# Channel mix of a fused three-stage kernel: where its operand parts are made, when its loads are issued, and the place of one relu

## The chip, the cores and the metric

The kernel runs on one core of a Trainium2 chip. The metric is the time of one execution on the device in microseconds (us), as the median of three runs. The engines are named as the profile names them: PE is TensorE's matmuls and PEld its weight loads, DVE is VectorE, ACT is ScalarE, SP is SyncE, whose queue issues nearly all DMAs. Each engine runs its own instructions in the order in which they were written for it, and waits where an operand of another engine, or a buffer, isn't there yet.

## The reference

Three layers in a row, all float32. The batch is 4 sequences of 3072 tokens, the model width 256.

```python
attn = np.maximum((1 / 3072) * z @ z.T, 0) ** 2          # d_qk 64
x = u * (attn @ v)
h = x @ w_in                                             # 256 -> 2048
x = (h - np.tanh(h)) @ w_out                             # 2048 -> 256
x_prev = x shifted by one token in its sequence, zero ahead of the first
xk = mu_k * x + (1 - mu_k) * x_prev
xr = mu_r * x + (1 - mu_r) * x_prev
k = np.maximum(xk @ w_k, 0)                              # 256 -> 1024
out = 1 / (1 + np.exp(-(xr @ w_r))) * (k * k @ w_v)      # 1024 -> 256
```

The last five lines are the channel mix.

## The kernel before

**Precision.** Every float32 operand of a matmul is held as two parts: a high part h, which ScalarE (line 87) or VectorE makes by a copy that rounds, and a low part l = value - h, which VectorE makes (line 90). A product is three matmuls: high times high, high times low, low times high (`PASSES`).

**Tiling.** Tokens go in 24 tiles of 512, features in chunks of 128. The channel mix takes two tiles at a time, t0 = 2i and t1 = 2i + 1, in 12 **groups**. A group is four **units** (j = 0 to 3, one `h_unit` each, called unit 0 to unit 3 here) and then an **r slot** (`r_slot`), 24 matmuls for the sigmoid's argument. Hidden products are made by a Winograd scheme: the four operands "own" B11, B12, B21, B22 (two tiles by two chunks of xk) and the differences T1 to T4 stand against weights A11, A12, S1 to S4 and -A22, seven products a unit. Of the operands, B11, T1, B22, T3, B21, T2 and T4 are needed as parts; B12 goes only into differences.

**A unit on TensorE** (line 724 the seven products, line 761 the pieces of the second matmul, against w_v, of the unit before): A11 x B11 into bank `wa`, A12 x B21 into bank `we`, a third of the pieces, S2 x T2, S1 x T1, more pieces, S4 x B22, S3 x T3, the rest of the pieces, and last -A22 x T4 on top of `wa`. Units 0 to 3 have 39, 45, 51 and 45 matmuls, the r slot 24: 204 a group.

**What stands between them.** ScalarE copies `wa` after A11 x B11 (`r<-wa`), VectorE adds `we` to it (line 824). ScalarE splits off the high part of the previous unit's hidden values (`h_Hy`), VectorE the low part (`l_Hy`). ScalarE copies `wa` and `we` after S2 and S1 (line 730, into `rc`). Then `run_steps` puts the **steps** that are due into VectorE's order, then `later_load` tasks issue DMAs. Then come VectorE's two additions of `we` and `wa` to `rc` (line 853), after S4 and S3: -A22 x T4 writes into `wa`, so TensorE can't start it before the second addition has read `wa`. Then `l_Hx`, and on ScalarE relu and square of `rc` (lines 740, 741) and of `wa` after -A22 x T4.

**The steps.** For each group, `k_groups` prepares the next group's operands in five lists, one for each unit and one for the r slot: `own` is a multiply-add on two loaded tiles (line 422), `minus` a difference (line 438), `part` a high copy on ScalarE and the low part on VectorE. `r_step` prepares xr for the group that is running: line 422, a copy (483) and a difference (90), one step in each unit. Two tiles of output of the group before are transposed (`out_turn`, line 928) and sent in eight DMAs each (line 934), the odd tile out of `ends` in unit 3, the even one as a step of the r slot. `mix_load` (lines 416, 417) loads the two tiles of an `own` or an `r_step`, one slot ahead; in the r slot the loads were written behind the steps.

**Queues and buffers.** All these DMAs go through SyncE's queue in the order written. A load waits for a free buffer, and every DMA takes one of eight completion counters in turn, so it also waits until the eighth DMA before it has landed.

Of the kernel before, what the change touches and what calls it, by code (L numbers as in the profile page):

```python
# [19 lines left out]
def relu2_attention__tanh_ffn__channel_mix_kernel(  # L20
# [406 lines left out]
    def k_groups(i):  # L427
# [13 lines left out]
        def part(n):  # L441
            t = st.pop(n)
            if n in ("B11", "B21"):
                if "h" not in st:
                    st["h"], st["l"] = p4(f"kh{i}", F32R), p4(f"kl{i}", F32R)
                k = 0 if n == "B11" else 1
                h, l = st["h"][:, k], st["l"][:, k]
            elif n == "B22" or not i:
                w = p4(f"kp{i}_{n}", F32R)
                h, l = w[:, 0], w[:, 1]  # L450
            else:
                key, k = ("T2", 0) if n == "T2" else ("T2", 1) if n == "T1" else ("T3", int(n == "T4"))
                key = "big" + key
                if key not in st:
                    st[key] = big(f"kt{i}_{key}").rearrange("p (b l t) -> p b l t", b=2, l=2)
                h, l = st[key][:, k, 0], st[key][:, k, 1]
            copy_hi(h, t)
            sub_lo(l, t, h)
            x[n] = (h, l)

# [6 lines left out]
        def q(n):  # L467
            return (0.7, lambda: part(n))

        return [  # L470
            [o("B11", t0, 0), o("B12", t1, 0), d("T1", "B12", "B11", True)],
            [q("B11"), o("B22", t1, 1), d("T3", "B22", "B12")],
            [d("T2", "B22", "T1", True), q("B22"), q("T1")],
            [q("T3"), o("B21", t0, 1), d("T4", "T2", "B21", True)],
            [q("T2"), q("B21"), q("T4")],
        ]
# [335 lines left out]
    def h_unit(n, q):  # L812
# [12 lines left out]
        if n:  # L825
            low = h_split("y")
            if "a" in hb:
                less(gx[:, 0], hb.pop("a"))
            low()
        if L == "H":  # L830
            tanh(gx[:, 1], r1)
            less(gx[:, 1], r1)
# [12 lines left out]
        for f in lates.pop(slot(n), ()):  # L845
            f()
# [10 lines left out]
        empty()  # L857
        if L == "H":
            tanh(gy, rc)
            less(gy, rc)  # L860
        else:
            relu2(gy, rc)
        hb["y"] = (n, 0, 2, ((n, 0, 1), (n, 1, 1)), gy)
        product(a, n, "-A22", "T4", False, True)
        if L == "H":
            tanh(gx[:, 0], a)
            hb["a"] = a
        else:
            relu2(gx[:, 0], a)
            for f in ends.pop(slot(n), ()):  # L870
                f()

    def h_end(n):
        gx = hb["g"][0]
        h_split("y")()
        hb["x"] = (n, 0, 1, ((n - 1, 1, 0), None), gx)
        h_split("x")()

    def r_slot(i, between):
# [13 lines left out]
        between()  # L893
        for t in (2 * i, 2 * i + 1):
# [57 lines left out]
    ends = {}  # L952
# [100 lines left out]
    for i in range(NT // 2):  # L1053
        n = NB + (NK + 1) * i
        first = n - NK - 1 if i else n - 8
        groups = {}

        def group(k, i=i, groups=groups):
            if not groups:
                groups["g"] = k_groups(i)  # L1060
            return groups["g"][k]

        for k in range(5):
            for t, c in ([(2 * i, 0), (2 * i + 1, 0)], [(2 * i + 1, 1)], [], [(2 * i, 1)], [])[k]:
                later_load(first + k - 1, mix_load, 0, t, c)
            task(first + k, first + k, group, k)
        for k in range(4):
            later_load(n + k - 1, mix_load, 1, 2 * i + k // 2, k % 2)
            task(n + k, n + k, lambda t, c: [(1.9, lambda: r_step(t, c))], 2 * i + k // 2, k % 2)
        n += NK + 1  # L1070
        if i < NT // 2 - 1:
            ends[n + 3] = [lambda c=c, t=2 * i + 1: out_turn(t, c) for c in range(DC)]
            task(n + 4, n + 4, lambda t: [(0.7, lambda c=c: out_turn(t, c)) for c in range(DC)], 2 * i)
# [25 lines left out]
    with tc.manual_schedule():  # L1099
# [45 lines left out]
        for n, (L, i, j) in enumerate(seq):  # L1145
# [4 lines left out]
            if L == "K" and j == NK - 1:  # L1150
# [4 lines left out]
                run_steps(m)  # L1155
                for f in lates.pop(m, ()):
                    f()
        n = len(seq) - 1
# [36 lines left out]
```

## Time and profile before

| | |
|---|---|
| median of 3 runs | 2628.63 us (2621.77 to 2632.17) |
| profiled execution | 2623.51 us |
| its span, first to last instruction | 2621.7 us |
| busy in the span: TensorE, VectorE, ScalarE | 96%, 75%, 69% |
| share of the chain that ended last: TensorE, VectorE, ScalarE, DMA | 15%, 4%, 2%, 2% |

The page gives one execution. Busy times are shares of the whole span, with three stages in it: attention up to about 950 us, the tanh layer up to about 1924 us, and the channel mix. In 40 slices of the span TensorE shows 9 (90% or more) up to slice 31 and 8 in the last nine, which lie in the channel mix. The engine rows of a stage are therefore read for that stage alone. In a timeline row the number in brackets is how long the engine sat idle before the row, and whose work ended that. A matmul's row is 0.39 us long while another starts every 0.23 us, since they overlap.

### The profile page before, as it was taken

How to read it: one execution, taken by the hardware profiler on the slowest of the kernel's cores; microseconds unless marked ns; L12 is line 12 of the kernel's file. 1: busy time of each engine (PE TensorE's matmuls, PEld its weight loads, DVE VectorE, ACT ScalarE, POOL GpSimd, SP SyncE). 2: the span in 40 equal slices, each digit the busy share in tenths (PEclk: the TensorE clock that was granted, in tenths of full speed). 3: DMA queues.
4: the chain of work that ended last, by engine and by line, in shares of the span. 5: the costliest groups of instructions: out<-in, count | busy, mean ns of one | idle time of the engine just before them, and what ended most of it. 6: DMA issues, size and time to landing. Idle time of an engine off the chain costs nothing. (4 is left out here: it accounts for less than half of the span.)

```text
span 2621.7 us, 30656 instructions
## 1 busy us (share of the span) xinstructions
PE 2523.3 (96%) x10907; PEld 2064.0 (79%) x10907; DVE 1974.1 (75%) x2650; ACT 1820.9 (69%) x2424; POOL 0.7 (0%) x5
## 2 busy tenths in 40 slices
PE   9999999999999999999999999999999888888888
PEld 7888888888888887888888888888877666676666
DVE  8888888888788777777777777777776666666665
ACT  7766875776687666676776776767777666666665
POOL 0000000000000000000000000000000000000000
PEclk9999999999999999999999999999999999999999
DMA  7798689679868931012110111102232333322233
GB/s 191 219 233 216 204 222 237 187 203 227 212 211 268 232 118 37 29 65 97 65 49 17 65 65 65 49 19 87 101 129 59 96 117 87 97 81 81 81 91 71
DMA packets 425145, 326.06 MB, mean 124 GB/s; under 512 B 270624, under 2 KB 344352, under 8 KB 424992
## 3 DMA queue, kind: packets, MB, share of 16 engines
q1 hardware_dynamic: 419712, 323.45, 43.3%
q8 instruction: 85, 1.39, 0.2%
q10 hardware_dynamic: 5280, 0.66, 0.2%
q14 instruction: 68, 0.56, 0.1%
HBM read 182.45 MB, written 135.54 MB: 121 GB/s over the span
## 5 line engine op out<-in xcount | busy, mean ns | idle before, releaser
L708 PE MATMUL acc_A<-h_A,v 128*128 128x512 f32 x1344 | 441.0, 390 | 0.0
L573 ACT ACTIVATE a_A<-w_A 128x1024 f32<-128x1024 f32 (+1 forms) x169 | 172.7, 1022 | 199.9 <-PE w_A L667 199.2
L708 PE MATMUL acc_A<-h_t,v 128*128 128x512 f32 x960 | 310.0, 389 | 0.0
L708 PEld LDWEIGHTS acc_A<-h_A,v 128*128 128x128 f32 x1344 | 253.1, 188 | 52.4
L761 PE MATMUL acc_H<-h_Hy,w_out 128*128 128x512 f32 x768 | 263.9, 389 | 0.0
L708 PE MATMUL acc_A<-l_A,v 128*128 128x512 f32 x672 | 262.4, 390 | 0.2 <-DVE l_A L90 0.2
L761 PE MATMUL acc_H<-h_Hx,w_out 128*128 128x512 f32 x768 | 252.2, 389 | 0.0
L90 DVE TENSOR_TENSOR l_A<-a_A,h_A 128x1024 fp32r<-128x1024 f32 (+1 forms) x169 | 201.8, 1194 | 64.4 <-ACT h_A L87 63.6
L724 PE MATMUL wa<-xo_T,w_in 128*128 128x512 f32 x864 | 243.4, 390 | 2.3 <-DVE rc L853 2.1
L824 DVE TENSOR_TENSOR r<-we,r 128x512 f32<-128x512 f32 x144 | 99.4, 690 | 155.9 <-PE we L724 86.6
L601 DVE STREAM_TRANSPOSE k<-a_A 128x512 f32<-128x512 f32 x240 | 155.9, 688 | 76.1 <-ACT a_A L574 75.4
L708 PEld LDWEIGHTS acc_A<-h_t,v 128*128 128x128 f32 x960 | 180.2, 188 | 37.4
L730 ACT ACTIVATE rc<-wa 128x512 f32<-128x512 f32 x144 | 86.0, 597 | 159.1 <-PE wa L724 159.0
L724 PEld LDWEIGHTS wa<-xo_T,w_in 128*128 128x128 f32 x864 | 161.6, 188 | 38.1 <-DVE rc L853 4.7
L708 PE MATMUL acc_A<-l_t,v 128*128 128x512 f32 x480 | 186.7, 389 | 0.0
L90 DVE TENSOR_TENSOR l_Hy<-g_H,h_Hy 128x1024 fp32r<-128x1024 f32 x144 | 175.6, 1219 | 9.7 <-ACT h_Hy L87 9.2
L574 ACT ACTIVATE a_A<-a_A 128x1024 f32<-128x1024 f32 (+1 forms) x169 | 178.4, 1056 | 5.4
L90 DVE TENSOR_TENSOR l_Hx<-g_H,h_Hx 128x1024 fp32r<-128x1024 f32 (+1 forms) x145 | 175.0, 1207 | 3.2 <-ACT h_Hx L87 3.0
L87 ACT ACTIVATE h_t<-b 128x512 fp32r<-128x512 f32 x240 | 137.1, 619 | 57.7 <-PE acc_A L708 53.7
L724 PE MATMUL wa<-kt_bigT,w_k 128*128 128x512 f32 x396 | 122.5, 420 | 55.9 <-DVE rc L853 55.9
L734 ACT ACTIVATE g_H<-rc 128x1024 f32<-128x1024 f32 x96 | 101.9, 1062 | 105.4 <-DVE rc L853 105.4
L761 PEld LDWEIGHTS acc_H<-h_Hy,w_out 128*128 128x128 f32 x768 | 144.2, 188 | 30.0 <-ACT h_Hy L87 0.2
(211 smaller groups left out, 5500.6 us busy)
## 6 DMA issues: line engine op xcount, KB each, us to landing
at<-k SPq DMA_DIRECT2D x120, 512.0 KB, 3.8
b<-at SPq DMA_DIRECT2D x240, 256.0 KB, 6.4
prevd<-pv SPq DMA_DIRECT2D x96, 256.0 KB, 2.3
mx<-x2d SPq DMA_DIRECT2D x96, 256.0 KB, 3.9
my<-prevd SPq DMA_DIRECT2D x96, 256.0 KB, 4.2
vr<-in_v_dram SPq DMA_DIRECT2D x24, 512.0 KB, 6.8
uin<-in_u_dram SPq DMA_DIRECT2D x192, 64.0 KB, 2.7
x1d<-uT SPq DMA_DIRECT2D x24, 512.0 KB, 3.4
```

Source lines behind the costliest of these rows:

```text
L87: nc.scalar.activation(out=o, in_=i, func=ACTF.Copy)
L90: nc.vector.tensor_tensor(out=o, in0=i, in1=hi.bitcast(F32), op=ALU.subtract)
L573: nc.scalar.activation(out=a[:, x], in_=w[:, x], func=ACTF.Relu, scale=sc)
L574: nc.scalar.activation(out=a[:, x], in_=a[:, x], func=ACTF.Square)
L601: nc.vector.transpose(out=t[:, :, :, c].rearrange("p b a j -> p a b j"), in_=a[:, c].rearrange("p (a b i) -> p a b i", a=4, b=4),)
L708: nc.tensor.matmul(o[c], w[j][a][:, c * P : (c + 1) * P], s[m][:, j], start=p == 0 and j == 0 and n == 0, stop=p == last and j == 1 and n ...
L724: nc.tensor.matmul(o, w[l][:, (j % 4) * P : (j % 4 + 1) * P], x[m], start=first and k == 0, stop=last and k == 2, skip_group_check=True,)
L730: nc.scalar.activation(out=t, in_=a, func=ACTF.Copy)
L734: nc.scalar.activation(out=g, in_=h, func=ACTF.Tanh)
L761: nc.tensor.matmul(o[c], w[a][:, f % 4, c * P : (c + 1) * P], hp[n, half, t][m], start=bool(first and k == 0), stop=bool(last and k == 2),)
L824: nc.vector.tensor_tensor(out=r1, in0=e, in1=r1, op=ALU.add)
```

## The change

1. `part` becomes `high` and `low`. The high copies of a unit are written behind its steps and its loads, ahead of `h_Hx`'s copy (`starts`); the low parts behind VectorE's two additions and `l_Hx` (`ends`). Parts are made in units 1, 2 and 3 (B11 and T1; B22 and T3; B21, T2 and T4), none in the r slot.
2. The differences go ahead: T3 and T2 in unit 1, T4 in unit 2. So three lists of steps remain in place of five, and the loads for them move with them.
3. `r_step`s: of the four, the first goes to the r slot before the group, and unit 1 has none (the first group keeps one in each unit).
4. The odd tile's transposes become steps of unit 3, ahead of the additions, with their eight DMAs. In the r slot the loads are written ahead of the steps, so ahead of the even tile's output transfers.
5. Relu and square of `wa` are written one unit later, behind `r<-wa` and `h_Hy`'s copy.

```diff
-        def part(n):
-            t = st.pop(n)
+        def high(n):
+            t = st[n]
...
             copy_hi(h, t)
-            sub_lo(l, t, h)
             x[n] = (h, l)
+
+        def low(n):
+            sub_lo(x[n][1], st[n], x[n][0])
...
         return [
             [o("B11", t0, 0), o("B12", t1, 0), d("T1", "B12", "B11", True)],
-            [q("B11"), o("B22", t1, 1), d("T3", "B22", "B12")],
-            [d("T2", "B22", "T1", True), q("B22"), q("T1")],
-            [q("T3"), o("B21", t0, 1), d("T4", "T2", "B21", True)],
-            [q("T2"), q("B21"), q("T4")],
-        ]
+            [o("B22", t1, 1), d("T3", "B22", "B12"), d("T2", "B22", "T1", True)],
+            [o("B21", t0, 1), d("T4", "T2", "B21", True)],
+            [],
+        ], high, low
...
             low()
+            if "relu" in hb:
+                relu2(gx[:, 0], hb.pop("relu"))
...
         run_steps(slot(n))
-        for f in lates.pop(slot(n), ()):
+        for f in lates.pop(slot(n), []) + starts.pop(slot(n), []):
             f()
...
         empty()
+        for f in ends.pop(slot(n), []):
+            f()
...
         else:
-            relu2(gx[:, 0], a)
-            for f in ends.pop(slot(n), ()):
-                f()
+            hb["relu"] = a
...
-        first = n - NK - 1 if i else n - 8
+        first = n - NK - 1 if i else n - 7
...
-        for k in range(5):
-            for t, c in ([(2 * i, 0), (2 * i + 1, 0)], [(2 * i + 1, 1)], [], [(2 * i, 1)], [])[k]:
+        for k in range(4):
+            for t, c in ([(2 * i, 0), (2 * i + 1, 0)], [(2 * i + 1, 1)], [(2 * i, 1)], [])[k]:
                 later_load(first + k - 1, mix_load, 0, t, c)
-            task(first + k, first + k, group, k)
-        for k in range(4):
-            later_load(n + k - 1, mix_load, 1, 2 * i + k // 2, k % 2)
-            task(n + k, n + k, lambda t, c: [(1.9, lambda: r_step(t, c))], 2 * i + k // 2, k % 2)
+            if k < 3:
+                task(first + k, first + k, group, k)
+            for x in ((), ("B11", "T1"), ("B22", "T3"), ("B21", "T2", "T4"))[k]:
+                starts.setdefault(first + k, []).append(lambda x=x, g=groups: g["g"][1](x))
+                ends.setdefault(first + k, []).append(lambda x=x, g=groups: g["g"][2](x))
+        for k, m in enumerate((-1, 0, 2, 3) if i else (0, 1, 2, 3)):
+            later_load(n + m - 1, mix_load, 1, 2 * i + k // 2, k % 2)
+            task(n + m, n + m, lambda t, c: [(1.9, lambda: r_step(t, c))], 2 * i + k // 2, k % 2)
         n += NK + 1
         if i < NT // 2 - 1:
-            ends[n + 3] = [lambda c=c, t=2 * i + 1: out_turn(t, c) for c in range(DC)]
-            task(n + 4, n + 4, lambda t: [(0.7, lambda c=c: out_turn(t, c)) for c in range(DC)], 2 * i)
+            for t, m in ((2 * i + 1, n + 3), (2 * i, n + 4)):
+                task(m, m, lambda t: [(0.7, lambda c=c: out_turn(t, c)) for c in range(DC)], t)
...
                 r_slot(i, lambda: h_end(n + 1) if final else None)
-                run_steps(m)
                 for f in lates.pop(m, ()):
                     f()
+                run_steps(m)
```

TensorE's order is the same in both kernels. The others are shown at three places of a middle group. Numbers in the names are those of the hidden products' units, counted through both layers (115 is unit 3 of a group, 116 and 117 are units 0 and 1 of the next), and of tiles (t = 6 to 13).

VectorE, from unit 3's `l_Hx` through the r slot to unit 0, before: the transposes `ot`, and low parts (line 90, `kt`, `kl`) that wait for ScalarE's copies.

```order
L90 TENSOR_TENSOR l_Hx115_17879<-g_H_8381,h_Hx115_17878 128x1024
L928 STREAM_TRANSPOSE ot7_17906<-sg7_17534 128x512 x2
L928 STREAM_TRANSPOSE ot6_17951<-sg6_17531 128x512
L90 TENSOR_TENSOR kt5_bigT2_17786<-kd5_T2_17781,kt5_bigT2_17786 128x512
L928 STREAM_TRANSPOSE ot6_17951<-sg6_17531 128x512
L90 TENSOR_TENSOR kl5_17693<-my0_10_1_17794,kh5_17692 128x512
L90 TENSOR_TENSOR kt5_bigT3_17872<-kd5_T4_17876,kt5_bigT3_17872 128x512
L824 TENSOR_TENSOR r1_116_17988<-we_116_17980,r1_116_17988 128x512
L90 TENSOR_TENSOR l_Hy115_17992<-g_H_8381,h_Hy115_17991 128x1024
L422 SCALAR_TENSOR_TENSOR my1_10_0_17969<-mx1_10_0_17968,head_63,my1_10_0_17969 128x512
```

VectorE at the same place now: the three low parts stand directly behind `l_Hx`, a first r step (`my1_10_0`, `mr10`) between the even tile's transposes.

```order
L90 TENSOR_TENSOR l_Hx115_17897<-g_H_8381,h_Hx115_17896 128x1024
L90 TENSOR_TENSOR kl5_17705<-my0_10_1_17701,kh5_17704 128x512
L90 TENSOR_TENSOR kt5_bigT2_17707<-kd5_T2_17694,kt5_bigT2_17707 128x512
L90 TENSOR_TENSOR kt5_bigT3_17799<-kd5_T4_17791,kt5_bigT3_17799 128x512
L931 STREAM_TRANSPOSE ot6_17973<-sg6_17541 128x512
L422 SCALAR_TENSOR_TENSOR my1_10_0_17890<-mx1_10_0_17889,head_63,my1_10_0_17890 128x512
L481 CAST mr10_17979<-my1_10_0_17890 128x512
L90 TENSOR_TENSOR mr10_17979<-my1_10_0_17890,mr10_17979 128x512
L931 STREAM_TRANSPOSE ot6_17973<-sg6_17541 128x512
L822 TENSOR_TENSOR r1_116_17996<-we_116_17988,r1_116_17996 128x512
L90 TENSOR_TENSOR l_Hy115_18000<-g_H_8381,h_Hy115_17999 128x1024
```

Both tiles' transposes and all low parts stood between `l_Hx115` and `r1_116` before; one tile's transposes and the first r step have taken the others' place.

SyncE's queue around the same r slot, before: 16 output DMAs, then the loads.

```order
L934 DMA out_0_dram<-ot7_17906 32x16x32 x8
L934 DMA out_0_dram<-ot6_17951 32x16x32 x8
L416 DMA mx1_10_0_17968<-x2d10_98 128x512
L417 DMA my1_10_0_17969<-prevd1_1_120 128x512
L416 DMA mx0_12_0_17972<-x2d12_100 128x512
L417 DMA my0_12_0_17973<-prevd0_2_117 128x512
L416 DMA mx0_13_0_17976<-x2d13_101 128x512
L417 DMA my0_13_0_17977<-prevd0_2_117 128x512
```

SyncE's queue there now, with the odd tile's transfers (`ot7`) from unit 3 and the even tile's (`ot6`) from the r slot:

```order
L937 DMA out_0_dram<-ot7_17875 32x16x32 x8
L416 DMA mx1_10_0_17889<-x2d10_98 128x512
L417 DMA my1_10_0_17890<-prevd1_1_120 128x512
L416 DMA mx1_10_1_17961<-x2d10_98 128x512
L417 DMA my1_10_1_17962<-prevd1_1_120 128x512
L416 DMA mx0_12_0_17965<-x2d12_100 128x512
L417 DMA my0_12_0_17966<-prevd0_2_117 128x512
L416 DMA mx0_13_0_17969<-x2d13_101 128x512
L417 DMA my0_13_0_17970<-prevd0_2_117 128x512
L937 DMA out_0_dram<-ot6_17973 32x16x32 x8
```

Eight output DMAs (the odd tile's, written in unit 3) stand ahead of the eight loads, and eight (the even tile's) behind them.

VectorE in unit 1, before: between `l_Hy` and the two additions (`rc`, line 853) stand an r step, a low part, an own operand, a difference and two multiplications for the output.

```order
L90 TENSOR_TENSOR l_Hy116_18073<-g_H_8381,h_Hy116_18072 128x1024
L422 SCALAR_TENSOR_TENSOR my1_10_1_18026<-mx1_10_1_18025,head_63,my1_10_1_18026 128x512
L483 CAST mr10_18017<-my1_10_1_18026 128x512
L90 TENSOR_TENSOR mr10_18017<-my1_10_1_18026,mr10_18017 128x512
L90 TENSOR_TENSOR kl6_18107<-my0_12_0_17973,kh6_18106 128x512
L422 SCALAR_TENSOR_TENSOR my0_13_1_18030<-mx0_13_1_18029,head_63,my0_13_1_18030 128x512
L438 TENSOR_TENSOR my0_13_0_17977<-my0_13_1_18030,my0_13_0_17977 128x512
L919 TENSOR_TENSOR sg8_17945<-acc_K8_17747,sg8_17945 128x512 x2
L853 TENSOR_TENSOR rc_117_18090<-we_117_18061,rc_117_18090 128x512
L853 TENSOR_TENSOR rc_117_18090<-wa_117_18062,rc_117_18090 128x512
```

VectorE in unit 1 now:

```order
L90 TENSOR_TENSOR l_Hy116_18074<-g_H_8381,h_Hy116_18073 128x1024
L422 SCALAR_TENSOR_TENSOR my0_13_1_18033<-mx0_13_1_18032,head_63,my0_13_1_18033 128x512
L438 TENSOR_TENSOR my0_13_0_17970<-my0_13_1_18033,my0_13_0_17970 128x512
L438 TENSOR_TENSOR kd6_T2_18108<-my0_13_1_18033,kd6_T1_18030 128x512
L922 TENSOR_TENSOR sg8_17955<-acc_K8_17756,sg8_17955 128x512 x2
L853 TENSOR_TENSOR rc_117_18093<-we_117_18062,rc_117_18093 128x512
L853 TENSOR_TENSOR rc_117_18093<-wa_117_18063,rc_117_18093 128x512
L90 TENSOR_TENSOR l_Hx117_18124<-g_H_8381,h_Hx117_18123 128x1024
L90 TENSOR_TENSOR kl6_18119<-my0_12_0_17966,kh6_18118 128x512
L90 TENSOR_TENSOR kt6_bigT2_18121<-kd6_T1_18030,kt6_bigT2_18121 128x512
```

The r step and the low part are gone from there, a second difference (`kd6_T2`) has come in; the low part of B11 (`kl6`) and that of T1 behind it come after `l_Hx117`.

## Rows read from the trace of the kernel before

**Rows 1.** Waits of TensorE, 1973.1 to 2599.2 us: total us, times, longest.

```profile
PE wa L724 <- DVE rc L853: 55.9, 30, 4.7
PE we L724 <- ACT kh L87: 11.5, 11, 1.0
PE we L724 <- DVE kl L90: 9.3, 11, 0.9
```

**Rows 2.** Engines by stretch: us, busy (instructions) of each, granted clock, DMA share, GB/s.

```profile
1973.10:2599.20 626.10, 549.42 (x2245) 435.83 (x2244) 417.85 (x592) 417.33 (x604) 0.00 (x0) 0.96 0.30 85
```

**Rows 3.** Timeline, TensorE, one group: start, us, line, tiles, count, [idle before <-releaser].

```profile
2206.25 0.39 PE L724 MATMUL wa<-kh,w_k 128*128 128x512 f32 x1
...
2208.13 0.50 PE L724 MATMUL we<-kh,w_k 128*128 128x512 f32 x1 [1.04 <-ACT kh L87]
2209.53 0.49 PE L724 MATMUL we<-kl,w_k 128*128 128x512 f32 x1 [0.90 <-DVE kl L90]
...
2221.74 0.97 PE L724 MATMUL wa<-kt_bigT,w_k 128*128 128x512 f32 x3 [3.04 <-DVE rc L853]
...
2234.18 0.96 PE L724 MATMUL wa<-kt_bigT,w_k 128*128 128x512 f32 x3 [1.90 <-DVE rc L853]
2234.98 0.40 PE L724 MATMUL wa<-kh,w_k 128*128 128x512 f32 x1
...
2245.89 0.84 PE L724 MATMUL wa<-kt_bigT,w_k 128*128 128x512 f32 x3
...
2256.97 0.96 PE L724 MATMUL wa<-kt_bigT,w_k 128*128 128x512 f32 x3 [0.72 <-DVE rc L853]
```

**Rows 4.** Timeline, SyncE's queue, output transfers of the same group.

```profile
2201.68 9.19 SPq L934 DMA_DIRECT2D out_dram<-ot  x16
```

**Rows 5.** DMA issues by line: count, KB each, median us from issue to landing.

```profile
my<-prevd SPq DMA_DIRECT2D x96, 256.0 KB, 4.2
```

**Rows 6.** Timeline, VectorE, same group: r slot, units 0 and 1.

```profile
2200.95 1.89 DVE L928 STREAM_TRANSPOSE ot<-sg 128x512 f32<-128x512 f32 x3
...
2215.28 0.75 DVE L422 SCALAR_TENSOR_TENSOR my<-mx,head,my 128x512 f32<-128x512 f32 x1 [2.94 <-DMA my<-prevd]
...
2219.00 0.75 DVE L422 SCALAR_TENSOR_TENSOR my<-mx,head,my 128x512 f32<-128x512 f32 x1 [1.05 <-DMA my<-prevd]
2219.79 0.69 DVE L438 TENSOR_TENSOR kd_T<-my,my 128x512 f32<-128x512 f32 x1
2220.40 0.68 DVE L853 TENSOR_TENSOR rc<-we,rc 128x512 f32<-128x512 f32 x1
2221.00 0.68 DVE L853 TENSOR_TENSOR rc<-wa,rc 128x512 f32<-128x512 f32 x1
...
2225.53 0.69 DVE L824 TENSOR_TENSOR r<-we,r 128x512 f32<-128x512 f32 x1 [1.52 <-ACT r L730]
2226.48 1.23 DVE L90 TENSOR_TENSOR l_Hy<-g_H,h_Hy 128x1024 fp32r<-128x1024 f32 x1 [0.26 <-ACT h_Hy L87]
2227.62 0.75 DVE L422 SCALAR_TENSOR_TENSOR my<-mx,head,my 128x512 f32<-128x512 f32 x1
...
2229.66 0.69 DVE L90 TENSOR_TENSOR kl<-my,kh 128x512 fp32r<-128x512 f32 x1
...
2232.85 0.68 DVE L853 TENSOR_TENSOR rc<-we,rc 128x512 f32<-128x512 f32 x1
```

**Rows 7.** Timeline, ScalarE, same group.

```profile
2207.46 0.62 ACT L87 ACTIVATE kh<-my 128x512 fp32r<-128x512 f32 x1
...
2223.77 0.58 ACT L740 ACTIVATE g_H<-wa 128x512 f32<-128x512 f32 x1
...
2224.92 0.58 ACT L730 ACTIVATE r<-wa 128x512 f32<-128x512 f32 x1
...
2234.16 1.06 ACT L740 ACTIVATE g_H<-rc 128x1024 f32<-128x1024 f32 x1 [3.59 <-DVE rc L853]
...
2256.95 1.06 ACT L740 ACTIVATE g_H<-rc 128x1024 f32<-128x1024 f32 x1 [2.39 <-DVE rc L853]
```

More of the change, by code (lines that the diff above doesn't have):

```diff
@@ L451, in part @@
             else:
-                key, k = ("T2", 0) if n == "T2" else ("T2", 1) if n == "T1" else ("T3", int(n == "T4"))
-                key = "big" + key
+                key = "big" + ("T2" if n in ("T1", "T2") else "T3")
                 if key not in st:
                     st[key] = big(f"kt{i}_{key}").rearrange("p (b l t) -> p b l t", b=2, l=2)
+                k = int(n in ("T1", "T4"))
                 h, l = st[key][:, k, 0], st[key][:, k, 1]
             copy_hi(h, t)
-            sub_lo(l, t, h)
             x[n] = (h, l)
+        def low(n):
+            sub_lo(x[n][1], st[n], x[n][0])
         def o(n, t, c):
@@ L465, in d @@
             return (0.7, lambda: minus(*y))
-        def q(n):
-            return (0.7, lambda: part(n))
         return [
             [o("B11", t0, 0), o("B12", t1, 0), d("T1", "B12", "B11", True)],
-            [q("B11"), o("B22", t1, 1), d("T3", "B22", "B12")],
-            [d("T2", "B22", "T1", True), q("B22"), q("T1")],
-            [q("T3"), o("B21", t0, 1), d("T4", "T2", "B21", True)],
-            [q("T2"), q("B21"), q("T4")],
-        ]
+            [o("B22", t1, 1), d("T3", "B22", "B12"), d("T2", "B22", "T1", True)],
+            [o("B21", t0, 1), d("T4", "T2", "B21", True)],
+            [],
+        ], high, low
     def r_step(t, c):
@@ L875, in h_end @@
         h_split("y")()
+        relu2(gx[:, 0], hb.pop("relu"))
         hb["x"] = (n, 0, 1, ((n - 1, 1, 0), None), gx)
@@ L893, in r_slot @@
         between()
+        if "relu" in hb:
+            relu2(hb["g"][0][:, 0], hb.pop("relu"))
         for t in (2 * i, 2 * i + 1):
@@ L951, in relu2_attention__tanh_ffn__channel_mix_kernel @@
     at = {x: n for n, x in enumerate(units)}
-    ends = {}
+    starts, ends = {}, {}
     loads, tasks = {}, []
@@ L1060, in group @@
                 groups["g"] = k_groups(i)
-            return groups["g"][k]
-        for k in range(5):
-            for t, c in ([(2 * i, 0), (2 * i + 1, 0)], [(2 * i + 1, 1)], [], [(2 * i, 1)], [])[k]:
+            return groups["g"][0][k]
+        for k in range(4):
+            for t, c in ([(2 * i, 0), (2 * i + 1, 0)], [(2 * i + 1, 1)], [(2 * i, 1)], [])[k]:
                 later_load(first + k - 1, mix_load, 0, t, c)
-            task(first + k, first + k, group, k)
-        for k in range(4):
-            later_load(n + k - 1, mix_load, 1, 2 * i + k // 2, k % 2)
-            task(n + k, n + k, lambda t, c: [(1.9, lambda: r_step(t, c))], 2 * i + k // 2, k % 2)
+            if k < 3:
[6 more added lines that the diff above has]
+            task(n + m, n + m, lambda t, c: [(1.9, lambda: r_step(t, c))], 2 * i + k // 2, k % 2)
         n += NK + 1
         if i < NT // 2 - 1:
-            ends[n + 3] = [lambda c=c, t=2 * i + 1: out_turn(t, c) for c in range(DC)]
-            task(n + 4, n + 4, lambda t: [(0.7, lambda c=c: out_turn(t, c)) for c in range(DC)], 2 * i)
+            for t, m in ((2 * i + 1, n + 3), (2 * i, n + 4)):
+                task(m, m, lambda t: [(0.7, lambda c=c: out_turn(t, c)) for c in range(DC)], t)
     tasks.sort(key=lambda x: x[:3])
```

## The prediction

> **What bounds the kernel now.** I read the page's slices first: TensorE is the full engine until the channel mix, and only there not. So I took that stage alone, from the first r slot to the last, 11 groups in 626.1 us, and asked in the waits view whom TensorE waits for in it [rows 1]: 55.9 us in 30 waits for VectorE's additions to `rc`, and 11.5 and 9.3 us in 11 waits each for B21's high and low part. VectorE and ScalarE are busy for 418 and 417 us of the 626, 38 us a group [rows 2], so neither is short of time; they are late at certain places. The timeline of one group shows which [rows 3]. In unit 0 A12 x B21 waits 1.04 us for `kh` and 0.90 us for `kl` (b); -A22 x T4 waits 3.04 us in unit 0 (c), 1.90 us in unit 1 (d), none in unit 2 (the row at 2245.89), 0.72 us in unit 3 (a).
>
> The stage's floor: from 2234.98 to 2245.89 TensorE starts 48 matmuls without a wait [rows 3], 0.2273 us each. 204 of them are 46.4 us a group, 510.1 us for eleven. The stretch has 116.0 us more. 76.7 us of it are the waits of rows 1. A wait's row starts at the modelled end of a matmul 0.39 us long, 0.16 us after the next could have started: 52 times 0.16 is 8.3 us. The mean granted clock is 0.96 [rows 2]; 4% of 626 us is 25 us, which stretches at 1.2 instead of 2.4 GHz take. 6 us are left, some 0.1 us of slow start behind each wait.
>
> **The change part by part,** in us from a unit's first matmul. Matmul m of a unit starts at 0.2273 x (m - 1), and its result is there some 0.45 us later (0.39 from [rows 3], and a short signal).
>
> (b) B21, T2 and T4 are parts of the r slot now. Their copies stand behind ScalarE's sigmoids (`kh`'s at 2207.46, 1.2 us after unit 0 has begun [rows 7]). In the new order they are made in unit 3: three copies of 0.62 us [rows 7] ahead of `h_Hx`, three low parts behind `l_Hx`. There ScalarE sits idle for 2.39 us ahead of `rc`'s relu [rows 7], and two copies come in addition, 1.24 us. The additions end at 8.5 there (as in unit 1, below), `h_Hx` somewhat later, `l_Hx` takes 1.2 and three low parts 1.8: the parts are ready some 12 us after unit 3's start, and unit 0 needs the first 45 + 24 matmuls after it, at 15.7. Both waits go.
>
> (c) In unit 0 VectorE waits 2.94 us for a load of the r step and 1.05 us for one of `own` [rows 6]. SyncE issues 16 output transfers for 9.19 us first [rows 4], and the loads stand behind them; a load lands 4.2 us after its issue [rows 5]. Now only two loads, those of the r step in the r slot, are behind eight outputs of unit 3; these end about 9.1 us after unit 3's start, so the loads land at about 14, and VectorE reaches that step at about 13. One us of waiting there has cover, since VectorE needs 0.63 us (a third of 1.89 [rows 6]) and 2.04 us for what is left in the r slot, and its next work for TensorE, `r`'s addition, can't begin before A12 x B21 is done, 1.6 us into unit 0, at 17.3. The other six loads follow by 12.7 and are wanted from 19.3 to 22: even at twice 4.2 us the last is there at 21.1. So no load is late. But the steps of unit 0 stay: an r step 2.04 (2227.62 to 2229.66), two `own` of 0.79 and a difference of 0.61 (2219.00 to 2220.40 [rows 6]), 4.2 in all. Unit 0's `r<-wa` starts when A11 x B11 is done, 0.9; with 0.58 for it [rows 7] and 1.05 for the `h_Hy` copy, `l_Hy` starts at 2.5 and takes 1.14 (2226.48 to 2227.62): the steps begin at 3.65 and end at 7.85. From the first addition to -A22 x T4 it is 1.34 (2220.40 to 2221.74 [rows 3, 6]), so TensorE can go on at 9.2; its 37th matmul could have started at 8.2. One us of wait stays, and I allow 0.1 for the slow start: 1.1 in place of 3.04 + 0.16 + 0.1.
>
> (d) In unit 1, 5.23 us of VectorE's order lie between the end of `l_Hy` and the first addition (2227.62 to 2232.85 [rows 6]). The r step goes (2.04) and so does `kl` (0.6), a difference comes (0.61): 3.2. Relu and square of `wa` take 1.15 us of ScalarE ahead of `r<-wa` (2223.77 to 2224.92 [rows 7]), and VectorE's `r` addition, `l_Hy` and steps hang on that copy (1.52 us of waiting at 2225.53); behind the copy they hold up nothing that TensorE wants within the unit. So the additions could come 3.2 us earlier. They are then bound by S3 x T3, the 33rd matmul, done at 7.75; with the second addition and its signal 8.5, and the 43rd matmul is due at 9.55. The wait of 1.90 goes, with 1.0 to spare. The low parts of this unit fall behind `l_Hx`, where VectorE had waited 1.52 us and more for `r<-wa`; two of 0.6 fit. ScalarE's two copies, one more than before, have 3.59 us of idle time (2234.16 [rows 7]).
>
> (a) In unit 3 two transposes of 0.63 us stand where a low part with its wait, an `own` and a difference stood, and ScalarE comes 1.15 us earlier: more than the 0.72 that is missing. Their eight transfers are issued while SyncE has nothing else due.
>
> Unit 2 has an `own` in place of two low parts ahead of its additions; it has no wait now and gets none.
>
> The sum: ten groups of the eleven prepare a successor and keep 1.1 us; the last has only (b), and keeps nothing. What was due to the clock goes with the waits that came before it; in rows 3 even the 1.90 us wait is followed by 48 matmuls at full speed, so I count none for one of 1 us. 116.0 - 10 x 1.1 = 105 us. For the first group, beside the tail of the tanh layer, I count nothing; as ScalarE has other work there, a gain there is between nothing and the 10 us of a steady group. The profiled execution took 2623.5 us: 2518.5 by this sum. Its time is 5.1 us below the median, 2628.6, so I put the median after at **2523 us**.
>
> **The rivals.**
> - *Loads still hold unit 0.* Eight loads in a row and eight outputs each wait until the eighth transfer before has landed, and for a buffer. If the six loads come late, (c) stays as it is. Of the 55.9 us, 7.2 are (a) and 19.0 (d), ten times each; 29.7 are left for (c), 31.3 with the 0.16, and with them about half of the 25 us of the clock. 2523 - 11 + 31 + 12 = 2555 us. For it: SyncE is a single queue in order. Against it: the 21.1 worked out above, and 19.3 as the first need.
> - *ScalarE becomes late.* Its copies stand ahead of `h_Hx` in units 1 to 3, which moves `h_Hx` to about 9.1 in unit 3, 0.7 behind the additions, and relu of `rc` and the next `r<-wa` with it. If all of that reached TensorE, 0.7 x 3 x 11 = 23 us: 2546 us. Against it: 38 us of work a group [rows 2] in 47.5.
> - *Slower.* The first r step of the next group is now in the r slot, ahead of `r`'s addition and `l_Hy` of unit 0 in VectorE's order, and its load is the first behind eight outputs. If it lands late, everything of unit 0 is late. From 0.6 us on (17.3 less 14 of arrival and 2.67 of work) each us costs ten a run. To end at 2642, 13 us slower than before, it must be 12.5 us late ((2642 - 2523) / 10 + 0.6), a landing of some 17 us against 4.2 [rows 5]; at 15 us late it would be 2523 + 144 = 2667 us.
> - *No change.* The wait may be one for room: `we`, `wa` and the loads rotate through few buffers, and an order that makes the same things earlier only waits for the same rooms. Then the time stays at 2629 us. Against it: in unit 1 VectorE works without a pause from 2227.62 up to the addition that TensorE waits for [rows 6]; what ends the wait is work. The Trainium skill ("Perfetto Trace Analysis", Optimization Strategy) says that consistent bubbles, the same gap repeating, can mean that there isn't enough SBUF or PSUM for the next tile. By that rule this change would give nothing; these rows speak for order, not for room.
>
> **How the numbers follow.** The forecast gets 0.70, loads that hold unit 0 0.15, a late ScalarE 0.08, no change 0.04, slower 0.03. A measurement of this kernel can tell about 0.5% from no change, 13 us. Forecast, loads and ScalarE are all faster by more: 0.93; same 0.04; slower 0.03. The forecast's own range is 2509 (no wait left in unit 0, and some gain in the first group) to 2541 (half of the second case); the two next cases end at 2555, and with the spread of the runs I take 2509 to 2558.
>
> **What would show it.** In the profile after: no TensorE wait for `kh` or `kl` in unit 0; at most one wait for `rc` a group, in unit 0, near 1 us, where the waits view now has 55.9 us; groups of about 47.5 us between r slots in place of 57; granted clock near 1.00 in the stage; VectorE waiting for no load in unit 0; `r<-wa` directly behind the square of `rc`. Wrong would be: waits for `my<-prevd` in the r slot of more than 2 us, `rc` waits in units 1 to 3, or a clock that stays at 0.96 though the waits are gone.

## The result, and the profile after

| | before | after |
|---|---|---|
| median (4 runs each) | 2629.07 us | 2514.72 us (2512.92 to 2517.76) |
| profiled execution | 2623.51 us | 2512.92 us |
| its span | 2621.7 us | 2511.1 us |
| first to last r slot | 626.1 us | 517.0 us |
| busy: TensorE, VectorE, ScalarE | 96%, 75%, 69% | 99%, 79%, 73% |

The ratio is 0.957, 95% interval 0.9548 to 0.9593. The forecast was 2523 us, from 2509 to 2558.

The waits of TensorE in the stretch from the first r slot to the last, which answer [rows 1] (line 853 is still the additions; line 722 is the products):

```profile
PE wa L722 <- DVE rc L853: 5.2, 10, 0.5
```

The same stretch by engine, which answers [rows 2] (start and end; busy us of PE, PEld, DVE, ACT, POOL; granted clock, DMA share, GB/s):

```profile
1973.00:2490.00 517.00, 511.83 (x2246) 420.42 (x2245) 422.30 (x592) 418.19 (x600) 0.00 (x0) 1.00 0.38 103
```

Of 76.7 us of waits 5.2 are left, one of 0.5 us in each of ten groups; VectorE and ScalarE are about as busy as they were (418 and 417 us before), and the granted clock went from 0.96 to 1.00. TensorE's unit 0 of the group whose r slot starts at 2161.28, which answers [rows 3]:

```profile
2166.72 0.39 PE L722 MATMUL wa<-kh,w_k 128*128 128x512 f32 x1
...
2174.66 0.39 PE L759 MATMUL acc_K<-h_Hy,w_v 128*128 128x512 f32 x1
2175.56 0.97 PE L722 MATMUL wa<-kt_bigT,w_k 128*128 128x512 f32 x3 [0.52 <-DVE rc L853]
```

VectorE in the r slot and in that unit 0, which answers [rows 6]:

```profile
2161.89 1.29 DVE L90 TENSOR_TENSOR kt_bigT<-kd_T,kt_bigT 128x512 fp32r<-128x512 f32 x2
...
2164.60 0.75 DVE L422 SCALAR_TENSOR_TENSOR my<-mx,head,my 128x512 f32<-128x512 f32 x1 [0.80 <-DMA my<-prevd]
...
2168.35 0.69 DVE L822 TENSOR_TENSOR r<-we,r 128x512 f32<-128x512 f32 x1 [1.19 <-PE we L722]
2169.18 1.23 DVE L90 TENSOR_TENSOR l_Hy<-g_H,h_Hy 128x1024 fp32r<-128x1024 f32 x1
2170.32 0.75 DVE L422 SCALAR_TENSOR_TENSOR my<-mx,head,my 128x512 f32<-128x512 f32 x1
...
2172.18 1.41 DVE L422 SCALAR_TENSOR_TENSOR my<-mx,head,my 128x512 f32<-128x512 f32 x2
2173.61 0.69 DVE L438 TENSOR_TENSOR kd_T<-my,my 128x512 f32<-128x512 f32 x1
2174.22 0.68 DVE L853 TENSOR_TENSOR rc<-we,rc 128x512 f32<-128x512 f32 x1
2174.82 0.68 DVE L853 TENSOR_TENSOR rc<-wa,rc 128x512 f32<-128x512 f32 x1
```

From 2169.18 to the second addition VectorE has no gap: the wait that is left for TensorE is for VectorE's work in unit 0. SyncE's queue around this r slot, which answers [rows 4] (the six loads between 2161.02 and 2163.82 are left out):

```profile
2155.41 4.96 SPq L937 DMA_DIRECT2D out_dram<-ot  x8
2160.42 0.51 SPq L416 DMA_DIRECT2D mx<-x2d  x1
...
2163.82 0.42 SPq L417 DMA_DIRECT2D my<-prevd  x1
2164.34 6.86 SPq L937 DMA_DIRECT2D out_dram<-ot  x8
```

All eight loads are out before the even tile's outputs. Groups are 47.07 us apart (2161.28 to 2208.34), where they were 53.6 to 58.8, and 46.24 for the last, which prepares no successor, where it was 50.4.

The one place without a gain is the first group, which lies ahead of the first r slot: that starts at 1973.0, as before (1973.1). The waits of TensorE from 1905 to there, first before, then after:

```profile
PE wa L724 <- DVE rc L853: 5.6, 4, 2.7
```

```profile
PE wa L722 <- DVE rc L853: 3.8, 2, 3.0
PE acc_K L759 <- ACT x L907: 2.0, 1, 2.0
```

### The profile page after: what moved, and what is told of

Its sections match the earlier page's. It is cut to its first block, busy times and chain, and to the rows that moved or that the text cites. A ratio compares the mean times of both kernels' runs of the same rounds, so it can differ in the third digit from the quotient of the medians.

```text
span 2511.1 us, 30719 instructions
## 1 busy us (share of the span) xinstructions
PE 2485.2 (99%) x10907; PEld 2048.1 (82%) x10907; DVE 1978.5 (79%) x2650; ACT 1823.9 (73%) x2424; POOL 0.7 (0%) x5
## 4 chain that ended last, share of the span: by engine, by line
PE 92%; DVE 3%; DMA 2%; ACT 1%; SPq 1%; issue 1%; DVEq 0%; ACTq 0%
PE acc_A L706 31%; PE acc_H L759 20%; PE wa L722 15%; PE we L722 11%; PE acc_K L759 7%; PE w_A L665 3%; PE w_A L664 3%; DMA out_dram<-ot 1%; DVE my L422 1%; SPq L937 1%; PE wa_r L889 1%; PE we_r L889 1%; DVE rc L853 1%; DMA mx<-x2d 0%; DMA my<-prevd 0%
## 5 line engine op out<-in xcount | busy, mean ns | idle before, releaser
L853 DVE TENSOR_TENSOR rc<-we,rc 128x512 f32<-128x512 f32 x144 | 99.1, 688 | 106.4 <-PE we L722 104.0
```

The lines of the kernel that those rows point to most:

```text
L853: nc.vector.tensor_tensor(out=rc[:, k], in0=x, in1=rc[:, k], op=ALU.add)
```

## Experiments: the change with one part undone

A kernel's ratio is to the kernel before, measured in the same series on the same chip. To see what an undone part costs, compare with 2514.72 us and with the 517.0 us between the r slots. The kernel before took from 2629.07 to 2632.67 us in the four series, so a difference of a few us between medians of two series shows nothing by itself; there the distance of the groups in the trace decides. Two parts of the change were not undone alone: the differences that go ahead, and the odd tile's transposes.

**Loads behind the outputs again.**

```diff
-                for f in lates.pop(m, ()):
-                    f()
                 run_steps(m)
+                for f in lates.pop(m, ()):
+                    f()
```

> The changed kernel, but in the r slot the loads are written behind the steps again, so six loads stand behind the even tile's eight outputs. Theory (c: the loads behind outputs held unit 0): in the profile after, these outputs take SyncE from 2164.3 to 2171.2, so the six loads are issued 2171.2 to 2174.0 in place of 2161.5 to 2164.2 and land some 4 us later; unit 0's steps end 3 to 5 us later, and its one wait for rc grows from 0.68 to 3 to 6 us. Ten times that and some lost clock: 2545 to 2580 us. Rival (the loads had cover anyway, moving the steps and parts did it all): under 2520 us, the wait in unit 0 still about 0.7.

Measured: 2571.57 us, ratio 0.9768 (0.9751 to 0.9786), 56.9 us more than the change. TensorE's waits from 1970 on, and the stage:

```profile
PE wa L722 <- DVE rc L853: 40.7, 11, 4.6
```

```profile
1976.70:2548.50 571.80, 531.11 (x2246) 434.31 (x2246) 424.98 (x592) 418.87 (x600) 0.00 (x0) 0.96 0.34 93
```

It is 54.8 us more between the r slots: 35.5 are a longer wait in unit 0 (40.7 - 5.2), and with the waits came the clock of before, 0.96. The loads had no cover behind the outputs.

**Every r step in its own unit again** (none in the r slot).

```diff
-        for k, m in enumerate((-1, 0, 2, 3) if i else (0, 1, 2, 3)):
+        for k, m in enumerate((0, 1, 2, 3)):
```

> The changed kernel, but every r step stands in its own unit again (units 0, 1, 2, 3; none in the r slot). Unit 0 keeps one r step, unit 1 gets one of 1.86 us. In the profile after, VectorE's second addition of unit 1 ends at 2184.8 and TensorE wants it at 2185.9, so 1.1 us are to spare. Theory (what holds TensorE is VectorE's work ahead of the additions of that unit): a second wait for rc in every group, in unit 1, of 0.7 to 0.9 us, ten times: 2521 to 2525 us. Rival (the r slot was the tight place, its load lands late): the waits stay as they are or unit 0's falls, 2505 to 2515 us.

Measured: 2523.87 us, ratio 0.9587 (0.9568 to 0.9606), 9.2 us more. Unit 1 on TensorE has the new wait, once in each of ten groups, beside the old one in unit 0:

```profile
2194.76 0.97 PE L722 MATMUL wa<-kt_bigT,w_k 128*128 128x512 f32 x3 [0.58 <-DVE rc L853]
```

0.58 and the 0.16 that a matmul's row hides are the 0.74 that 1.86 us of work against 1.1 us of room should give. In unit 0 nothing changed, though the r slot was lighter: the r slot isn't the tight place. Groups are 47.97 us apart, 0.9 more than 47.07.

**Low parts ahead of the additions again.**

```diff
+        for f in ends.pop(slot(n), []):
+            f()
         product(e, n, "S4", "B22", False, True)
...
         empty()
-        for f in ends.pop(slot(n), []):
-            f()
```

> The changed kernel, but the low parts stand ahead of VectorE's two additions, where they wait for ScalarE's high copies. From the profile after: in unit 3 the third high copy ends at 2206.2, so the third low part would end at 2206.9 and the second addition at 2208.2, against 2207.6 when TensorE wants it: 0.6 us late; unit 1 0.1 to 0.2 late; unit 2 not. Theory (their place counts, by less than a us a group): waits for rc in unit 3 and unit 1, some 0.8 us more a group, 2521 to 2527 us. Rival (low parts ahead cost nothing, the units have room): 2513 to 2517 us.

Measured: 2528.23 us, ratio 0.9607 (0.9591 to 0.9623), 13.5 us more; groups of 48.17 us, 1.1 more each. VectorE and TensorE at the end of unit 3:

```profile
2216.20 0.69 DVE L855 TENSOR_TENSOR rc<-we,rc 128x512 f32<-128x512 f32 x1
2216.80 0.68 DVE L855 TENSOR_TENSOR rc<-wa,rc 128x512 f32<-128x512 f32 x1
```

```profile
2217.54 0.97 PE L722 MATMUL wa<-kt_bigT,w_k 128*128 128x512 f32 x3 [0.54 <-DVE rc L855]
```

Of the 1.1 us a group, 0.8 lie at this place: 0.54 of wait, the 0.16 that a matmul's row hides and 0.13 of slow start. The other 0.3 lie in unit 1, where -A22 x T4 starts 0.14 us late, too little to show as a wait, and the matmul behind it 0.14 more. The expectation had 0.8 in all. The first r slot starts 4.4 us later too (1977.4), but that can't be put down to the low parts: it starts at 1976.7 with the loads behind the outputs, an edit that changes nothing ahead of it.

**Relu and square right behind -A22 x T4 again.**

```diff
-            hb["relu"] = a
+            relu2(gx[:, 0], a)
...
-        relu2(gx[:, 0], hb.pop("relu"))
```

> The changed kernel, but relu and square of wa stand right behind -A22 x T4 again, ahead of the next unit's copy of wa. They take 1.2 us, and unit 1 has 1.1 us to spare. Theory (the parts of the change cover each other: with the r step and a low part gone from unit 1, the place of relu is worth nearly nothing): a wait of 0 to 0.3 us in unit 1, none in units 2 and 3, 2513 to 2519 us. Rival (it is a part of its own, worth what it takes): 1.2 us in one or two units of every group, 2526 to 2540 us.

Measured: 2517.03 us, ratio 0.9563 (0.9548 to 0.9578), 2.3 us more by the medians, but the intervals of the ratios overlap. The groups are 47.27 us apart in place of 47.07. In the full change this part is worth 0.2 us a group.

## Experiments: one part alone on the kernel before

**Only the parts of B21, T2 and T4 out of the r slot** (`part` gives its low part back as a function; other lines left out).

```diff
-            [q("T2"), q("B21"), q("T4")],
...
+        lows = starts.pop(slot(n))() if slot(n) in starts else []
         hb["x"] = (n, 0 if n else 1, 2, ((n - 1, 1, 0) if n else None, (n, 0, 0)), gx)
...
         low()
+        for f in lows:
+            f()
```

> The kernel before, with one thing changed: B21, T2 and T4 are made into parts in unit 3 (high copies ahead of h_Hx's copy, low parts behind l_Hx), not in the r slot. Theory (the wait that ends last in unit 0 is the load): the waits for kh and kl, 20.8 us, go, but VectorE still waits for the same loads, so -A22 x T4 waits as much longer as TensorE comes earlier: 2615 to 2630 us. Rival (the waits add up, each is worth its own time): 2.2 us a group and a share of the clock, 2592 to 2604 us.

Measured: 2662.57 us, ratio 1.013 (1.011 to 1.0149): 33 us slower than before. Neither expectation had that size: the theory ended at 2630 us. TensorE's waits, VectorE in unit 0, and SyncE ahead of it, in the group whose r slot starts at 2274.54:

```profile
PE wa L726 <- DVE rc L856: 116.9, 32, 9.8
```

```profile
2277.39 2.48 DVE L933 STREAM_TRANSPOSE ot<-sg 128x512 f32<-128x512 f32 x4
...
2291.72 0.75 DVE L422 SCALAR_TENSOR_TENSOR my<-mx,head,my 128x512 f32<-128x512 f32 x1 [8.04 <-DMA my<-prevd]
```

```profile
2278.12 9.32 SPq L939 DMA_DIRECT2D out_dram<-ot  x16
2287.48 0.51 SPq L416 DMA_DIRECT2D mx<-x2d  x1
```

The waits for `kh` and `kl` went, and no time with them: these 20.8 us of waits lay ahead of the load that unit 0 waits for anyway. And the three low parts, behind an `l_Hx` that waits 0.76 us for ScalarE, now stand ahead of the odd tile's transposes. So the sixteen outputs start 3.6 us after the r slot's start (2278.12 - 2274.54) in place of 0.9 (2201.68 [rows 4] against 2200.77), and the loads behind them 2.8 us later. The slow start after the longer wait lies in the open too: the granted clock is 0.50, the lower level of 1.2 GHz, where before such a stretch lay behind the `kl` wait, ahead of the wait for the load, and was covered by it. The first row is TensorE's in the kernel before, in unit 0 (0.63 us for one matmul, not 0.39), the others are stretches of the new kernel, the wait and what follows it:

```profile
2210.21 0.63 PE L761 MATMUL acc_K<-h_Hx,w_v 128*128 128x512 f32 x1
```

```profile
2288.20:2297.18 8.98, 0.11 (x1) 0.00 (x1) 5.23 (x9) 0.02 (x1) 0.00 (x0) 0.63 0.97 323
2297.18:2300.60 3.42, 3.42 (x8) 2.74 (x9) 2.28 (x3) 3.36 (x5) 0.00 (x0) 0.50 0.21 82
```

**Only the loads ahead of the steps in the r slot.** The edit is the first one of this document, the other way round.

> The kernel before, with one thing changed: in the r slot the loads are written ahead of the steps, so ahead of eight of the sixteen outputs. Theory: VectorE's waits for loads in unit 0, 2.94 and 1.05 us, shrink to under 1 us, and -A22 x T4 of unit 0 waits 0 to 1.2 us in place of 3.04; the waits for kh and kl stay: 2 to 3 us a group and a share of the lost clock, 2588 to 2610 us. Rival (without the parts out of the r slot VectorE comes no earlier, and the wait moves): 2620 to 2630 us.

Measured: 2583.44 us, ratio 0.9829 (0.981 to 0.9848), 46 us less than before and 4.6 us below the theory's range. The waits for `kh` and `kl` stay at 11.5 and 9.3 us; those for `rc` halve:

```profile
PE wa L724 <- DVE rc L853: 27.9, 24, 1.9
```

In unit 0 VectorE has no load to wait for; it is ready before TensorE:

```profile
2201.31 1.41 DVE L422 SCALAR_TENSOR_TENSOR my<-mx,head,my 128x512 f32<-128x512 f32 x2
...
2203.91 0.69 DVE L853 TENSOR_TENSOR rc<-we,rc 128x512 f32<-128x512 f32 x1 [0.46 <-PE we L724]
```

Of the three parts that were tried alone it is the only one that is worth much by itself.

**Only relu behind the copy.** The edit is that of the fourth experiment, the other way round.

> The kernel before, with one thing changed: relu and square of wa are written behind the next unit's copy of wa and h_Hy's copy. Theory (VectorE's order ahead of the additions hangs on that copy): the wait of 1.90 us in unit 1 falls to about 0.75, that of 0.72 in unit 3 goes, units 0's stay; 1.9 us a group and a share of the clock, 2598 to 2612 us. Rival (VectorE's steps alone fill unit 1): 2620 to 2630 us.

Measured: 2627.73 us, ratio 1.000 (0.9986 to 1.0014), the rival's time. ScalarE's copy and VectorE's r step come 1.15 us earlier, as meant, and then VectorE waits for as long:

```profile
2226.43 0.69 DVE L90 TENSOR_TENSOR kl<-my,kh 128x512 fp32r<-128x512 f32 x1 [1.22 <-ACT kh L87]
```

The low part `kl` is next in VectorE's order, and its high copy stands on ScalarE behind the copies of `rc`, which come when TensorE has done S1 x T1. Here moving the relu gains nothing while a low part stands ahead of the additions.

**Both: parts out of the r slot and loads ahead of the steps.**

> The kernel before with both of the last two edits: B21, T2 and T4 made into parts in unit 3, and in the r slot the loads ahead of the steps. Alone the first gave 2662.6 us and the second 2583.4. Theory (they cover for each other: without the parts in the r slot TensorE reaches -A22 x T4 of unit 0 some 3.4 us earlier, and only with early loads is VectorE there too): the waits for kh and kl are gone, -A22 x T4 of unit 0 waits 0.5 to 2.5 us, units 1 and 3 as before (2.08 and 0.88): 2555 to 2580 us. Rival (what the first cost comes from its place in unit 3 and stays): 2610 us and more.

Measured: 2622.03 us, ratio 0.9965 (0.9952 to 0.9978), 38.6 us more than the loads alone by the medians, 36 by the ratios. The rival's number came. The rows of SyncE:

```profile
2205.69 4.13 SPq L939 DMA_DIRECT2D out_dram<-ot  x8
2209.87 0.52 SPq L416 DMA_DIRECT2D mx<-x2d  x1
```

With the r slot at 2202.1, the odd tile's eight outputs still start 3.6 us behind it, and the loads follow them; in nine groups -A22 x T4 of unit 0 waits 4.4 to 5.4 us. In the full change the odd tile's transposes are steps of unit 3, ahead of the additions, and its outputs start 5.9 us ahead of the r slot (2155.41 against 2161.28). So the early loads alone don't make the parts in unit 3 pay. That the early transposes are what was missing is read from these rows; no run adds them alone.

## Experiments: the slower rival, and what was left

**The r step's load last in the r slot**, in place of first.

```diff
+            if m < 0:
+                behind[n - 1] = lambda t=2 * i: mix_load(1, t, 0)
+            else:
-            later_load(n + m - 1, mix_load, 1, 2 * i + k // 2, k % 2)
+                later_load(n + m - 1, mix_load, 1, 2 * i + k // 2, k % 2)
...
                 for f in lates.pop(m, ()):
                     f()
+                if m in behind:
+                    behind[m]()
                 run_steps(m)
```

> The changed kernel, but the two loads of the r step that stands in the r slot are the last of that slot's eight and not the first: they are issued 2.85 us later. This tests the slower rival of the prediction, a late first load. In the profile after, VectorE begins that step at 2164.6, 0.80 us after it could, and then still waits 1.19 us for TensorE ahead of r's addition. Theory (from 0.6 to 1.2 us on, each us costs one in every group): unit 0's wait grows by 1.5 to 2.3 us, ten times, and some clock: 2528 to 2545 us. Rival (more cover than that): under 2520 us.

Measured: 2545.18 us, ratio 0.9674 (0.9657 to 0.9691), 30.5 us more than the change. The r slot starts at 2176.93 here. VectorE, and TensorE's waits:

```profile
2185.96 0.75 DVE L422 SCALAR_TENSOR_TENSOR my<-mx,head,my 128x512 f32<-128x512 f32 x1 [6.51 <-DMA my<-prevd]
...
2188.45 0.65 DVE L822 TENSOR_TENSOR r<-we,r 128x512 f32<-128x512 f32 x1
```

```profile
PE we L722 <- DVE r L822: 21.5, 9, 3.3
PE wa L722 <- DVE rc L853: 5.3, 6, 1.0
```

```profile
2176.81 0.49 SPq L416 DMA_DIRECT2D mx<-x2d  x1
...
2179.78 0.38 SPq L416 DMA_DIRECT2D mx<-x2d  x1
```

The last rows are SyncE's first load of the slot and the first of the pair. The step began 9.0 us after the r slot's start, not 3.3 (2164.60 - 2161.28). The time came out at the theory's upper end, the place did not. TensorE now waits ahead of S1 x T1, since bank `we` is free only when `r`'s addition has read it; its waits for `rc` come to as much as in the change (5.3 us in six, where it was 5.2 in ten).

**T1 in unit 1** in place of unit 0, on the change.

```diff
-            [o("B11", t0, 0), o("B12", t1, 0), d("T1", "B12", "B11", True)],
-            [o("B22", t1, 1), d("T3", "B22", "B12"), d("T2", "B22", "T1", True)],
+            [o("B11", t0, 0), o("B12", t1, 0)],
+            [d("T1", "B12", "B11", True), o("B22", t1, 1), d("T3", "B22", "B12"), d("T2", "B22", "T1", True)],
```

> The changed kernel, with the difference T1 as the first step of unit 1 in place of the last step of unit 0. VectorE's work ahead of unit 0's additions falls by 0.61 us, where TensorE waits 0.68 and loses 0.11 more; in unit 1 it rises by 0.61, where 1.1 us are to spare. Theory (what is left is VectorE's work in unit 0 and nothing else): waits of 0.1 us or none in unit 0, none in unit 1, 6 to 8 us less than the changed kernel, 2505 to 2510 us. Rival (unit 0 is bound by something else too, a load or a copy of ScalarE, or unit 1 has no room): 2512 to 2518 us.

Measured: 2503.17 us, ratio 0.9524 (0.9506 to 0.9542). Between the r slots TensorE doesn't wait at all:

```profile
1972.50:2481.80 509.30, 509.30 (x2245) 420.47 (x2244) 419.97 (x592) 417.36 (x600) 0.00 (x0) 1.00 0.39 105
```

517.0 - 509.3 is 7.7 us for ten waits of 0.68 us, each with a slow start of 0.11. The spans differ by 8.3 us (2511.1 and 2502.8); the other 3.2 of the 11.5 us between the medians come from the choice of profiled runs: that of the change lies 1.8 us under its median, this one's 1.5 us above.

**The split of w_r one unit later,** with T1 in unit 1, in the first group.

```diff
-    load(n + 1, lambda: half_load(("r", 0), wd["r", 0][:, 0]))
-    task(n + 2, n + 2, half_steps, ("r", 0), r_room)
+    load(n + 2, lambda: half_load(("r", 0), wd["r", 0][:, 0]))
+    task(n + 3, n + 3, half_steps, ("r", 0), r_room)
```

> The changed kernel with T1 in unit 1, and the split of w_r one unit later, in unit 3 of the first group in place of unit 2. There VectorE waits 3.2 us for ScalarE's copy of w_r, which stands behind four copies of x2, and TensorE waits 3.1 us for the additions behind it. Theory: that wait and the slow clock behind it go, some 3 to 5 us less than 2503.2: 2498 to 2500. Rival (VectorE's r step in that unit waits for its load or for a buffer just as long): 2502 to 2505 us.

Measured: 2501.37 us, ratio 0.9506 (0.949 to 0.9522), the fastest kernel here, between the two expectations. The first r slot starts 3.0 us earlier than with T1 alone (1969.5 against 1972.5); the medians differ by 1.8 us, within their intervals. In the first group the longest wait for the additions is 1.6 us, in unit 3, where the split now is and VectorE waits 2.6 us for ScalarE's copy of w_r, in place of 3.0 in unit 2:

```profile
PE wa L722 <- DVE rc L853: 2.5, 2, 1.6
PE acc_K L759 <- ACT x L907: 0.5, 1, 0.5
```

**And the first group's first r step in the tanh layer.**

```diff
-        for k, m in enumerate((-1, 0, 2, 3) if i else (0, 1, 2, 3)):
+        for k, m in enumerate((-1, 0, 2, 3) if i else (-4, 0, 2, 3)):
```

> As the kernel with w_r one unit later, and the first group's first r step four units earlier, in the tanh layer, so that unit 1 of the first group has none. Theory: the first group's wait of 1.2 us for rc in unit 1 goes too; the one for the copies of x2 (1.4 us) stays or grows by as much, since TensorE comes earlier: 2496 to 2500 us. Rival (the r step holds up the tanh layer's unit): 2500 us and more.

Measured: 2503.56 us, ratio 0.9512 (0.9497 to 0.9528), the rival's time. The wait for the additions in unit 1 went, and the one for ScalarE's copies of x2 is 3.0 us in place of 0.5: the first group has another bound there. How much of the growth this edit made isn't shown, since that wait differs between profiles of the same first group: 2.0 us in the change, 3.0 with its loads behind the outputs.

```profile
PE acc_K L759 <- ACT x L907: 3.0, 1, 3.0
```

## Why the prediction held, and where it didn't

**The size.** Between the r slots 109.1 us went (626.1 - 517.0), 105 were forecast. Ten waits cost 7.9 us, not 11: +3.1. The floor was 46.3 us a group, not 46.4, as the kernel with no waits shows (509.3 / 11): +1. Behind the last r slot 1.4 us went (22.5 to 21.1), which the sum didn't have; no run looked at why. The profiled run of after lies 1.8 us under its median, that of before 5.6 us under its own: 3.8, which is the spread of the runs and no merit of the sum. Together these are 9.3 us, and the medians moved by 114.35.

**(c), the loads: right, and the mis-sized term of the sum.** The outputs of unit 3 end 9.3 us after its start (9.1 forecast), the r step starts at 13.5 (arrival at 14), having waited 0.80 us, which has cover (one us was allowed). The slot's last load is issued at 12.7 (12.7). What stays in unit 0 came out as its own sum said: steps from 3.60 (3.65 forecast) to 7.50 (7.85), -A22 x T4 at 8.84 (9.2), due at 8.17. The 0.35 us less is 0.18 for the r step (1.86 us where a row of before gave 2.04), 0.15 for two `own` (1.43 us, not 1.58) and the earlier start. Moving T1 out of this unit then removed the wait: it was work, not a load or room.

**(d) and (a): the waits went; the reason for part of (d) was wrong.** Unit 1 has 1.1 us to spare (2185.9 against an addition that ends at 2184.8), 1.0 was forecast. But the 1.15 us that I gave to the relu don't count alone: on the kernel before it gains nothing, and undoing it costs 0.2 us a group. VectorE waited for `kl`'s high copy next, 1.22 us. The waits view of before names the wait that ends last; what is next behind it has to be found in both engines' orders.

**(b): right for the whole, wrong as a term.** The parts are ready 12.1 us after unit 3's start (12 forecast), and the waits for `kh` and `kl` are gone. But the prediction counted 20.8 us of them among 116 us to be won. Alone, this part makes the kernel 33 us slower: the waits, and the slow clock behind them, lay under the wait for the load, and the low parts push the transposes, the outputs and the loads back. Even with the early loads it costs 38.6 us; in the full change, where the transposes are early too, the waits are gone at no such cost.

**The clock: right.** The granted clock is 1.00 in the stage, where it was 0.96, so the stretches at the lower level left with the waits.

**The first group: nothing, as counted, but for another reason.** A gain between nothing and 10 us was given, since ScalarE has other work there. In fact waits changed place: four for additions, 5.6 us, became two, 3.8 us, and one of 2.0 us for ScalarE's copies of x2. The run that moved the split of w_r shows that the longest, 3.0 us, came from it; the last run shows that the copies of x2 are a bound of their own. The trace names what they wait for: in the change ScalarE's copy sits idle for 1.12 us until a DMA that stores `pv` (x2 scaled for the shifted token) into `prevd` has landed, and for 2.01 us in the last run. No run changed that.

```profile
1945.81 0.60 ACT L907 ACTIVATE x<-acc_H 128x512 f32<-128x512 f32 x1 [1.12 <-DMA prevd<-pv]
```

**The rivals.** *Loads still hold unit 0* was priced at 2555 us; with the loads behind the outputs the change takes 2571.6. The mechanism was real, and its price is higher: TensorE's wait in unit 0 was 3.9 to 4.6 us in nine groups and not 3.04, as nothing ahead of it is waited for any more, and the clock's whole loss was back (0.96), where half was counted. *Slower* was real too, but overpriced and in another place. With the step at 5.7 us later its rule, ten a run for each us from 0.6 on, gives some 46 us ((13.5 + 5.7 - 14 - 0.6) x 10); 30.5 were measured. The cover is 1.19 us ahead of `r`'s addition and 1.08 us from its end (2169.04) to S1 x T1 (2170.12), which needs bank `we`. *A late ScalarE* did not show in the time: VectorE waits 0.62 us for `h_Hx` in unit 3, near the 0.7 that the rival had, but behind the additions, and TensorE waits for nothing there. *No change* was weighed on the Trainium skill ("Perfetto Trace Analysis", Optimization Strategy): the same gap repeating can mean too little room. Here the same gap repeated in every group, and the runs removed it by order alone, with the buffers as they were.

## What to carry to other kernels

Before a wait is counted as something to win, ask which wait on the same engine comes after it and what sets the end of that one: where the end of the later one doesn't depend on the earlier, as here with a load, taking the earlier away gains nothing until the later is moved. In an in-order DMA queue the place of a transpose decides when a load behind its output starts, so moving VectorE's work moves loads (by 2.8 us here). An experiment that makes each part alone shows which parts are conditions for others: here the parts alone gave +33, -46 and -2 us, together with the moved differences, transposes and r step -114.

## What the runs showed of the hardware

The prediction let the clock's loss go with the waits that came before it. It is less regular: after an idle 2.98 us in the first group of after TensorE got 0.53 for the next 3.39 us; after an idle 2.74 us in the kernel with only the relu moved it got 1.00.

```profile
1957.40:1960.38 2.98, 0.02 (x2) 0.00 (x1) 2.89 (x5) 2.65 (x5) 0.00 (x0) 1.00 0.77 283
1960.38:1963.77 3.39, 3.39 (x8) 2.62 (x9) 2.43 (x3) 2.71 (x5) 0.00 (x0) 0.53 0.96 292
```

```profile
2215.80:2218.54 2.74, 0.00 (x2) 0.01 (x1) 2.70 (x5) 0.02 (x1) 0.00 (x0) 1.00 1.03 394
2218.54:2222.00 3.46, 3.46 (x15) 2.87 (x16) 2.96 (x4) 3.43 (x4) 0.00 (x0) 1.00 0.06 21
```

No run here separates what decides between the two. The other surprise is the queue: measured from the r slot, a pair of loads that was issued 3.7 us later (2.85 in place of -0.86) was there 5.7 us later, behind six other loads of 256 KB each. Why it lost another 2.0 us wasn't tried.
